# Per-chunk state product of an mLSTM in (128,32) column tiles, run together with the gather

## The chip, the cores and the metric

The kernel runs on one core of a Trainium2 chip. The metric is device time in microseconds (us) for one execution, taken as the median of three runs. TensorE is called PE, VectorE DVE, ScalarE ACT, GpSimd POOL; SP is SyncE, whose queue issues nearly all DMAs. "L902" is line 902 of the kernel before.

## The reference

An mLSTM layer (4 batches, 8 heads, 768 steps, head size 40) feeds a gated feed-forward network over 3072 tokens (320 to 1536 to 320):

```
for t in range(S):
    m_new = maximum(f[t] + m, i[t])
    C = exp(f[t] + m - m_new) * C + exp(i[t] - m_new) * outer(v[t], k[t])     # 40 x 40 per head
    n = exp(f[t] + m - m_new) * n + exp(i[t] - m_new) * k[t]
    y[t] = sigmoid(o[t]) * (C @ q[t]) / maximum(abs(n . q[t]), 1)
x = y laid out as (batch * step, head * 40)
out = (sigmoid(x @ w_gate) * (x @ w_val)) @ w_out
```

## The kernel before

The 768 steps are taken in 6 chunks of 128 tokens. A chunk c of a batch b is a unit, number 4c + b, 24 in all. Within a unit the recurrence is three matrix products. The *scores* (`b` in the order, L771/L776) are k·q per head, 128x128, which DVE multiplies with a decay matrix (`bm`, L782). The *gather* (`c`, L754) is scores times v: 8 heads, each cut by `by_columns` into four matmuls whose 32 columns of weights lie in one of the four column tiles of the array, 32 matmuls in all, with 41 columns of v each (40 and a column of ones for the normaliser n). *Into* (`ci`, L797) is q times the state that the chunks before left; it is faded (`cf`, L801) and added to the gather (`cs`, L810), and normalisation and the output gate follow (`cg` to `cx`).

The state of a batch is `cst[:, b]`, three groups of three, three and two heads. In each group the state stands as a block-diagonal matrix of 120x123 (the last 80x82), so that one *into* matmul serves a whole group. At the end of a unit of chunks 0 to 4 (20 units) it is brought up to date, in `st_e`:

- `z` (L902): three matmuls, v against the weighted k, give 120x123, 120x123 and 80x82 into a PSUM bank of their own, "cs". The products of different heads lie beside the diagonal blocks.
- `zm` (L913 on ACT, one piece per head column, or L917 on DVE): copies them out and multiplies with a mask `rmask` that keeps the blocks on the diagonal.
- `zd` (L896, POOL or DVE): the old state times the chunk's decay `cdec`; `za` (L922): the masked product is added. Both come in two parts (two groups, and the last).

The weighted k is `kt` times the last column of the decay matrix (`bk`, L757). From unit 8 on q and k go another way to PE: DVE flips them (`a`), splits them into a high part (`ah`, L697/L699) and a low part (`al`, L702), SP writes those to DRAM scratch (`as`, L706), reads q back as the weights of *into* (`aq`, L713, three transfers `qk`) and both back as stacked operands of the scores (`s`, L741). The decay matrices come from DRAM too (`ld`, L482).

The feed-forward takes 128 tokens at a time. All operands are split in a high and a low part in fp32r. Its up matmuls (`t`, `pg`, L951: 256 or 512 columns) fill PSUM, ACT and DVE make tanh and product (`ta` L964, `tg` L967), these are split again (`th` L972/L974, `tl` L978), and the down matmuls (`p`, `po`, L989, 320 columns) follow.

Nothing is scheduled while the kernel runs: all steps are put under keys, and a string ORDER lists the keys. Steps are issued in that order, each on its engine, and an engine runs its steps in that order alone. PSUM banks of the attention steps alternate between two; each is free again when its reader is done.

Of the kernel before, what the change touches and what calls it, by code (L numbers as in the profile page):

```python
# [9 lines left out]
F32 = mybir.dt.float32  # L10
F32R = mybir.dt.float32r
# [112 lines left out]
d1 w3b gc dy0 iq w3d wrf g dx1 lv2 a2.0 w3e w5a dy1 w7a g t0 w5b ah2.0 t0 lq4 t0 w5b t0 e2a w5b z0 t0 w7b t0*2 w7b
w5d a3.0 g e2m t0 zm0.0 t0 ah3.0 t0*5 zm0.1 w6a t0 w7b / a3.1 g ta0 w5e t0 w4f a2.2 ah3.1 gcs bk2 t1 tg0 t1*3 w6b
lo2 t1 th0 t1 v3 h0 t1 g t1 e3 t1*2 w6b t1*3 h0c t1 tl0 lo3 p0 t1 w6b t1 w4a / b2.0 ah2.2 w4b p0 ta1 p0 w4b b2.2
w7d g w4b p0 w7e t2 bm2.0 w6d t2 w7f t2*3 tg1 lv3 t2 e3a p0 bm2.2 b2.1 w5f w6e ld4 a3.2 w8a bm2.1 t2 e3m t2*2 ct2
t2 ah3.2 c2 th1 w8b w4d v6 bk3 b3.1 cg2 cv2 tl1 t2 cv2 t2 bm3.1 t2 w9a t2 p1 t2 w4e cv2 ct3 t2 / b3.0 cr2 ta2 w8b
cx2 p0 w9b b3.2 bm3.0 p1*2 bm3.2 t3*2 w8b z2 w9b w8d w8f p1 zm2.0 d2 zm2.1 w9b t3 w8e t3 dx2 tg2 c3 w9f w9d dy2 lk4
t3 w9e cg3 p1 gs t3*2 th2 cv3 z3 cv3 wvf gc w11a cv3 tl2 t3*2 w6f cr3 t3 zm3.1 t3*2 w11b lq5 t3 zm3.0 t3 cx3 t3 g  # L130
d3 lk5 t3 ta3 p2*2 dx3 p1 tg3 p2*2 w12a g p2 dy3 p2 k0 th3 t4 w12b t4*2 w11b k0c t4 ie w13a tl3 t4*2 w11b t4*2 e4
t4*5 p3 t4 w13b t4 w12b t4 a4.2 w13b ta4 p3 w12b p3 ah4.2 a4.1 w13b t5 w12d w14f t5 aq4.2 t5 tg4 t5 w12f t5 a4.0
ah4.1 w11d t5 lv4 w12e v5 t5*2 th4 t5 ld5 t5 w11e t5 ah4.0 t5*2 w10a lo4 t5*2 tl4 p4*2 w10f ci4 w10b ta5 aq4.0 e4a
p4 t5 p4 w10b p4 t6 tg5 t6 p4 w10b t6 w13d t6 e4m lo5 t6*3 cf4 t6 w10d t6*2 b4.2 th5 t6*2 w15a t6 bk4 lq6 tl5 t6*3
p5 bm4.2 p3*2 w10e p3 v4 p5 ta6 k0 b4.0 tg6 k0d t7 th6 t7 k0d t7 w13e w14a t7*2 tl6 t7 bm4.0 t7 w18a t7 p5 t7 w14b
t7*2 aq4.1 t7 p5 t7*2 k0d t7 w18b t7 p5 w14b ta7 p5 / a5.0 w18b z4 w14b ah5.0 w18b t8 w13f b4.1 g w18d w14d w15b t8
w18e lk6 e5a t8 tg7 t8 w18f t8 th7 t8 w14e zm4.0 p6*2 bm4.1 zm4.1 t8 w15f p6 w16a w15b t8 lq8 p6 t8 w15b e5 t8 gs
t8 w16b t8*2 tl7 t8*2 / h1 ta8 c4 h1c w16b*2 p6 v7 t8 p7*2 cs4 e5m a5.2 t9 tg8 ah5.2 t9 w17a p6 p7 t9 th8 w17b t9
w17b t9 w15d aq5.0 t9*2 w17b t9*2 tl8 w17d w17f t9*2 w11f w15e / a5.1 t9 gs ah5.1 t9 cv4 bk5 ct4 t9 w16f aq5.1 p7
cv4 w16d p7 cg4 p7 gs t9 cv4 p8 t9 cr4 ta9 w17e p8*3 w22a / a6.0 tg9 t10 ah6.0 p8 b5.0 w22b w19a w16e t10*2 th9 t10  # L140
w22b t10 w22b p8 t10 w19b k1 w22f tl9 p8 ld7 k1c t10 w22d bm5.0 p8 ld6 t10*2 w19b w21a t10*3 w21b t10*2 w22e t10 p9
w19b p9 w20a t10 w21b / k1 w19f ta10 p9 w20b p9 lq10 p9*2 zd4.0 w19d p8 lv5 p8 w20b p9 w19e p9 tg10 lo7 p8 p9 p8 p9
w20b t11 th10 t11*2 a8.0 w20d b5.1 tl10 w24a t11 bm5.1 t11*2 w20e t11*3 ah8.0 p10 w21b t11 p10*3 w21d w20f p10 t11
w24b p10 lk7 p10 w21e k1d p10 t11 k1d t11 k1d cx4 t11*3 al8.0 ta11 p9*2 / ci5 w23a zd4.1 aq5.2 t12 w25a cf5 a6.2
t12 tg11 zd5.1 t12*3 w23b th11 t12 w25b t12 ah6.2 ct5 t12 w23b t12 e6 w24b t12 w23b d4 w24b b5.2 w27f tl11 t12 w24d
w23f t12 w23d t12 w25b t12 bm5.2 t12 w23e lq7 p11 dx4 t12 ta12 p11 p10 dy4 w24e p11 ct7 p11*2 tg12 w26a p11*2 p10
zd5.0 p10 p11 w26b p11 th12 aq6.0 / c5 t13 cs5 ld8 a6.1 za4.1 p10 as8.0 ah6.1 p11 cv5 w25b t13 w27a t13*2 za4.0
w25d t13 tl12 t13 / z5 w25e w27b p12 t13 zm5.1 lk9 t13 p12 as8.3 t13 w29a t13 w27b t13 cg5 t13 cv5 t13 cv5 t13 cr5
p12*3 w27b p12 cx5 p11 w26b p11 w27d w24f t13 zm5.0 p12 as8.2 w26b ci6 w27e ta13 as8.1 aq6.2 p12 w26d lo6 t13 t14*2
tg13 t14 d5 w26e t14 dx5 t14 lq11 t14 za5.0 th13 t14 za5.1 t14 lo8 w29b w28a t14 cf6 t14*2 tl13 t14*2 aq6.1 t14 aq8  # L150
t14 lq9 w28b t14 w29b ta14 p12 aq8 p13 zd6.0 a7.2 w28b p13 lv6 ah7.2 p13 tg14 e6a p12 t15 lv9 t15 dy5 p12 p13*2
a9.1 p13 e7a lq12 / b6.0 e6m w28b p12 b6.1 ah9.1 bk6 e8 th14 p13*2 t15*2 al9.1 t15 bm6.1 t15 e7 t15 w29b t15 tl14
# [24 lines left out]
p30 aq11 e12a p30 tg32 p30 lo11 t33*2 th32 t33*2 s11 zm10.1 t33 a12.1 p31 tl32 p31 s11 p31 p32 s11 p32 ci10 as12.1
# [1030 lines left out]
```

## Time and profile before

| what | value |
|---|---|
| median of three runs | 515.25 us (515.25 to 515.4) |
| span of the profiled execution | 511.8 us |
| own time of that execution (taken as the median) | 515.25 us, 3.45 us of it outside the span |
| PE busy | 503.7 us, 4671 matmul records |
| DVE, ACT, POOL busy | 318.6, 200.8, 164.3 us |
| mean DMA rate | 148 GB/s |

The span is what the profiler's rows cover; an execution's time contains some us before and behind it. An fp32 matmul stands in the trace as two records, so the gather's 32 matmuls are 64 records. Matmuls are pipelined: a record's duration runs from its start to its result, and the next starts before that. What a matmul costs PE is therefore the distance from its start to the next one's start. The chain of waits follows the execution back from its last instruction, at each step to what released it.

### The profile page before, as it was taken

The page shows a single profiled execution, that of the slowest core. Times are in us where ns is not written, and L with a number is a line of the kernel's source. Part 1 is how long each engine was busy: PE and PEld are TensorE (multiplying, and loading weights), DVE is VectorE, ACT ScalarE, POOL GpSimd, SP SyncE. Part 2 cuts the span into 40 slices and gives each one's busy share as a digit, 9 for nine tenths or more (in the row PEclk, how much of TensorE's full clock was granted, in tenths as well). Part 3 has the DMA queues.
Part 4 walks back from the last instruction along what each step waited for, and adds up shares of the span by engine and source line. Part 5 has one row for each costly group of instructions (what it writes and reads, how often), then busy time and mean ns, then how long its engine had stood idle before and what let it go on. Part 6 is the DMA issues. An engine that isn't in the chain of part 4 may idle for free.

```text
span 511.8 us, 12224 instructions
## 1 busy us (share of the span) xinstructions
PE 503.7 (98%) x4671; PEld 458.4 (90%) x4671; DVE 318.6 (62%) x767; ACT 200.8 (39%) x530; POOL 164.3 (32%) x226
## 2 busy tenths in 40 slices
PE   7899999999999999999999999999999999999997
PEld 6788988889999999988888888888888888999997
DVE  8899998997647667565867366676444434442222
ACT  5987765674423332353332322213432411222321
POOL 3563334557730231342225322432241311101111
PEclk9999999999999999999999999999999999999999
DMA  9997768789889695977887788769759730000000
GB/s 196 240 274 192 200 192 221 168 141 189 191 179 172 136 216 119 199 150 156 186 161 180 146 189 195 160 127 190 165 118 198 155 87 5 27 28 1 28 0 27
DMA packets 227578, 75.55 MB, mean 148 GB/s; under 512 B 207040, under 2 KB 215424, under 8 KB 227520
## 3 DMA queue, kind: packets, MB, share of 16 engines
q1 hardware_dynamic: 226432, 74.51, 66.4%
q8 instruction: 37, 0.61, 0.5%
q10 hardware_dynamic: 1088, 0.26, 0.3%
q14 instruction: 21, 0.17, 0.1%
HBM read 57.61 MB, written 17.14 MB: 146 GB/s over the span
## 4 chain that ended last, share of the span: by engine, by line
PE 94%; DVE 3%; DMA 1%; issue 0%; ACT 0%; SPq 0%; DVEq 0%; ACTq 0%
PE pg L951 53%; PE po L989 25%; PE av L754 3%; PE in L797 3%; PE s L776 2%; PE s L771 2%; PE cs L902 2%; PE xt L867 1%; DVE gin L1178 1%; DMA gin<-in_f_gate_dram 1%; DMA st<-in_moe_w_val_dram 1%; PE s L1105 0%; PE pt L639 0%; DVE dc L548 0%; DVE x L842 0%
## 5 line engine op out<-in xcount | busy, mean ns | idle before, releaser
L964 ACT ACTIVATE sg<-pg 128x256 f32<-128x256 f32 (+1 forms) x103 | 48.3, 469 | 221.5 <-PE pg L951 214.8
L967 DVE SCALAR_TENSOR_TENSOR sg<-sg,pg 128x256 f32<-128x256 f32 (+1 forms) x103 | 53.7, 522 | 106.1 <-ACT sg L964 62.7
L951 PE MATMUL pg<-xh,wh 128*128 128x256 f32 (+1 forms) x412 | 112.2, 336 | 0.0
L951 PE MATMUL pg<-xl,wh 128*128 128x256 f32 (+1 forms) x412 | 109.6, 332 | 0.1
L951 PE MATMUL pg<-xh,wl 128*128 128x256 f32 (+1 forms) x412 | 106.2, 329 | 0.0
L978 POOL TENSOR_TENSOR gl<-sg,gh 128x256 fp32r<-128x256 f32 (+1 forms) x51 | 48.9, 958 | 178.2 <-ACT gh L972 61.3
L989 PE MATMUL po<-ol,gh 128*128 128x320 f32 x288 | 87.6, 316 | 0.0
L989 PE MATMUL po<-oh,gh 128*128 128x320 f32 x288 | 87.6, 315 | 0.0
L989 PE MATMUL po<-oh,gl 128*128 128x320 f32 x288 | 86.9, 318 | 0.0
L951 PEld LDWEIGHTS pg<-xl,wh 128*128 128x128 f32 x412 | 70.5, 188 | 6.7 <-DVE xl L880 0.3
L951 PEld LDWEIGHTS pg<-xh,wl 128*128 128x128 f32 x412 | 69.2, 188 | 5.4
L951 PEld LDWEIGHTS pg<-xh,wh 128*128 128x128 f32 x412 | 70.0, 188 | 4.3 <-ACT sg L964 0.5
L951 PE MATMUL pg<-xl,w 128*128 128x256 f32 (+1 forms) x206 | 60.7, 331 | 0.0
L989 PEld LDWEIGHTS po<-oh,gl 128*128 128x128 f32 x288 | 53.2, 188 | 3.2
L989 PEld LDWEIGHTS po<-oh,gh 128*128 128x128 f32 x288 | 53.3, 188 | 3.0
L989 PEld LDWEIGHTS po<-ol,gh 128*128 128x128 f32 x288 | 53.3, 188 | 2.8
L951 PE MATMUL pg<-xh,w 128*128 128x256 f32 (+1 forms) x206 | 54.4, 329 | 0.0
L782 DVE TENSOR_TENSOR d<-s,d 128x384 f32<-128x384 f32 (+1 forms) x66 | 33.1, 506 | 23.1 <-PE s L776 20.3
L972 ACT ACTIVATE gh<-sg 128x256 fp32r<-128x256 f32 (+1 forms) x58 | 28.8, 497 | 42.5 <-DVE sg L967 33.4
L490 ACT ACTIVATE d<-d,at 128x128 f32<-128x128 f32 x136 | 42.8, 390 | 0.0
L951 PEld LDWEIGHTS pg<-xl,w 128*128 128x128 f32 x206 | 36.7, 188 | 2.2
L951 PEld LDWEIGHTS pg<-xh,w 128*128 128x128 f32 x206 | 35.1, 188 | 2.8
(153 smaller groups left out, 712.9 us busy)
## 6 DMA issues: line engine op xcount, KB each, us to landing
d<-mscr SPq DMA_DIRECT2D x22, 512.0 KB
k<-in_k_dram SPq DMA_DIRECT2D x24, 160.0 KB
v<-in_v_dram SPq DMA_DIRECT2D x24, 160.0 KB
o<-in_o_gate_dram SPq DMA_DIRECT2D x24, 160.0 KB
st_o<-in_moe_w_out_dram SPq DMA_DIRECT2D x12, 320.0 KB
scr0q<-qt SPq DMA_DIRECT2D x32, 120.0 KB
scr1q<-qt SPq DMA_DIRECT2D x32, 120.0 KB
out_dram<-ob SPq DMA_DIRECT2D x24, 160.0 KB
```

What stands on the lines that cost most here:

```text
L490: nc.scalar.activation(d[:, h, :], d[:, h, :], AF.Exp, bias=at[:, c, b * H + h : b * H + h + 1], scale=-1.0)
L754: nc.tensor.matmul(dst[xs], lhs[:, xs], rhs, start=True, stop=True)
L771: nc.tensor.matmul(ps[g][:, :nh, :], sop[u][:r, g, 0, :], sop[u][:r, g, 1 : 1 + nh, :], start=True, stop=True)
L776: nc.tensor.matmul(ps[g][:, m, :], ks[: 3 * D, h0 + m, :], qs[: 3 * D, h0 + m, :], start=True, stop=True)
L782: nc.vector.tensor_tensor(x, ps[g][:, :nh, :], x, ALU.mult)
L797: nc.tensor.matmul(pi[:, h0 : h0 + nh, :], qk[u][:r, g, :], cst[:r, b, g, : nh * DA], start=True, stop=True)
L951: nc.tensor.matmul(pg[x], w[:, a, fs] if a < 2 else w[:, fs], y[c][:, a, n0:n1], start=first, stop=a == 2 and y is xl)
L964: nc.scalar.activation(sg[0], pg[0], AF.Tanh, scale=0.5)
L967: nc.vector.scalar_tensor_tensor(sg[0], sg[0], 1.0, pg[1], ALU.add, ALU.mult)
L972: nc.scalar.activation(gh[u][:, :nt], sg[0], AF.Copy)
L978: E('gl0' if c == 0 else 'gl', f'tl{n}').tensor_tensor(gl[u][:, :nt], sg[0], gh[u][:, :nt].bitcast(F32), ALU.subtract)
L989: nc.tensor.matmul(po[t], g[c, j, t0][:, (t - t0) * P : (t - t0 + 1) * P], o[:, j, :], start=j == 0 and first, stop=j == NF - 1 and last)
```

## The change

The state is kept differently. `pair_state(b)` is 128 x 4 x 41: heads (0,3,6,2) stand in the upper 64 rows, heads (1,4,7,5) in the lower 64, four side by side; 24 of every 64 rows hold leftovers of neighbouring heads that nothing reads. The product becomes `outer`: 16 matmuls, each with 32 columns of the weighted k as weights and 41 columns of v, which write 32 rows of one head into one column tile. There are no products of different heads that must be masked.

For chunks 1 to 4 (16 units) `outer` follows in the same step as the gather's 32 matmuls and writes behind them in the same PSUM bank. For chunk 0 (4 units) it stays a step of its own, and a copy (`zm`) takes it out. `zd` is one operation of 128x164 on POOL, `za` one on DVE which reads PSUM directly; masks and their temporaries are gone.

*Into* still reads a block-diagonal matrix, now `cb`, which `zi` fills with zeros once (a POOL memset of 128x1476). `moved` copies the diagonal blocks there from the pair state: four transfers on SP per unit, 80 in all, `zs` in the order (two of 40x3x41, two of 40x41). `cdec` is made by copies, without the mask. In ORDER the first 113 words stand as before and the others are laid anew.

```diff
+PAIRS = ((0, 3, 6, 2), (1, 4, 7, 5))
+MOVES = ((0, 0, 0, 0, 3), (1, 1, 0, 0, 3), (2, 0, 3, 0, 1), (2, 1, 3, 1, 2))
...
-    cst = const.tile([P, B, 3, 3 * DA], F32, name="cst")
+    cb = const.tile([P, B, 3, 3 * DA], F32, name="cb")
...
+    def outer(u, dst):
+        for p in range(4):
+            for w in range(2):
+                for e in range(2):
+                    h = PAIRS[e][p]
+                    x0 = h * D - e * (64 - D) + 32 * w
+                    r0 = 64 * e + 32 * w
+                    nc.tensor.matmul(dst[r0 : r0 + 32, p, :], kt[u].rearrange("p h d -> p (h d)")[:, x0 : x0 + 32],
+                                     vt[u][:, h, :], start=True, stop=True)
...
-                nc.tensor.matmul(pi[:, h0 : h0 + nh, :], qk[u][:r, g, :], cst[:r, b, g, : nh * DA], start=True, stop=True)
+                nc.tensor.matmul(pi[:, h0 : h0 + nh, :], qk[u][:r, g, :], cb[:r, b, g, : nh * DA], start=True, stop=True)
...
         def gather():
-            t["pv"] = pv = bank(c, b, [P, H, DA], "av")
+            x = bank(c, b, [P, 12, DA], "av")
+            t["pv"], t["po"] = pv, po = x[:, :H, :], x[:, H:, :]
             for h in range(H):
                 by_columns(pv[:, h, :], dm[u][:, h, :], vt[u][:, h, :], PARAM['AV'])
+            if 0 < c < NCH - 1:
+                outer(u, po)
+
+        def fade():
+            x = pair_state(b)
+            E('cd', f'zd{n}').tensor_tensor(x, x, cdec[:, c - 1, b].unsqueeze(2).broadcast_to([P, 4, DA]), ALU.mult)
+
+        def added():
+            x = pair_state(b)
+            nc.vector.tensor_tensor(x, x, t["po"], ALU.add)
...
+        def moved(j, e, p0, g0, g1):
+            nc.sync.dma_start(cb[j * D : (j + 1) * D, b, g0:g1, j * DA : (j + 1) * DA],
+                              pair_state(b)[88 * e : 88 * e + D, p0 : p0 + g1 - g0, :])
```

In the rows of the order below, numbers behind a name are chunk, batch and a buffer's number; `x2` means twice in a row.

**Unit 4 and its state product.** PE in the kernel before; `cs_1_0` is the product's bank, `av_1_0` the gather's, `pt` the transposes of the next unit's q and k:

```order
L989 MATMUL po3_0_987<-oh_109,gl_0_1_2_1024 128x320
L639 MATMUL pt0_1_1_1085<-ident_94,k_1_1_845 120x128
L644 MATMUL pt0_1_1_1085<-ident_94,qpad0_89 120x128
L902 MATMUL cs_1_0_1089<-v_1_0_939,k_1_0_793 120x123 x2
L902 MATMUL cs_1_0_1089<-v_1_0_939,k_1_0_793 80x82
L951 MATMUL pg0_0_4_0_1099<-xh_0_435,wh0_103 128x512
L771 MATMUL s1_1_0_1104<-kq_1_0_910 128x384
L951 MATMUL pg0_0_4_0_1099<-xh_0_435,wh0_103 128x512
```

PE in the changed kernel:

```order
L951 MATMUL pg0_0_4_0_1147<-xl_0_467,w20_103 128x512
L646 MATMUL pt2_1_1_1195<-ident_93,k_1_1_971 80x128
L651 MATMUL pt2_1_1_1195<-ident_93,qpad0_89 80x128
L761 MATMUL av_1_0_1198<-v_1_0_1064,d_1_0_837 32x41 x32
L629 MATMUL av_1_0_1198<-v_1_0_1064,k_1_0_856 32x41 x16
L951 MATMUL pg1_0_4_0_1171<-xl_0_467,w21_106 128x512
L989 MATMUL po3_0_1010<-ol_108,gh_0_2_2_1101 128x320
```

The three wide matmuls stood between transposes and the next tile's `pg`, in a bank of their own; now 16 narrow ones follow the gather's 32 with nothing between them.

**Unit 2, the gather behind the scores.** PE in the kernel before; `s0`, `s1` and `s2` are the scores of heads 0 to 2, 3 to 5, and 6 and 7:

```order
L771 MATMUL s1_0_2_631<-kq_0_2_431 128x384
L639 MATMUL pt2_0_3_638<-ident_94,k_0_3_364 80x128
L642 MATMUL pt2_0_3_638<-ident_94,qpad1_90 80x128 x2
L951 MATMUL pg1_0_2_0_645<-xh_0_435,wh1_106 128x256 x2
L951 MATMUL pg1_0_2_0_645<-xh_0_435,wl1_107 128x256 x2
L754 MATMUL av_0_2_653<-v_0_2_418,d_0_2_301 32x41 x32
```

PE in the changed kernel:

```order
L951 MATMUL pg0_0_2_0_630<-xl_0_467,wh0_101 128x256
L778 MATMUL s1_0_2_643<-kq_0_2_439 128x384
L951 MATMUL pg0_0_2_0_630<-xl_0_467,wh0_101 128x256
L778 MATMUL s2_0_2_653<-kq_0_2_439 128x256
L951 MATMUL pg1_0_2_0_661<-xh_0_443,wh1_104 128x256
L761 MATMUL av_0_2_665<-v_0_2_426,d_0_2_299 32x41 x32
L951 MATMUL pg1_0_2_0_661<-xh_0_443,wh1_104 128x256
```

The last scores ahead of the gather were `s1`, with three transposes and four `pg` matmuls behind them; now they are `s2`, with one `pg` matmul behind them.

**Unit 9, the weights of its *into*.** SP in the kernel before; `qk_2_1` are the three transfers of q, `scr0q` and `scr0k` writes to scratch for unit 10:

```order
L1009 DMA out_0_dram<-ob_0_1_2076 128x320
L706 DMA scr0q_85<-qt_2_2_2088 32x30x32 x2
L713 DMA qk_2_1_2202<-scr1q_87 40x3x128 x2
L706 DMA scr0q_85<-qt_2_2_2088 32x30x32
L713 DMA qk_2_1_2202<-scr1q_87 40x2x128
L706 DMA scr0q_85<-qt_2_2_2088 32x30x32
L1009 DMA out_0_dram<-ob_0_2_2250 128x320
```

SP in the changed kernel:

```order
L720 DMA qk_2_1_2462<-scr1q_87 40x3x128 x2
L713 DMA scr0k_86<-kt_2_2_2345 32x20x32
L923 DMA cb_109<-cst_412 40x41
L713 DMA scr0k_86<-kt_2_2_2345 32x20x32
L923 DMA cb_109<-cst_412 40x3x41
L923 DMA cb_109<-cst_412 40x41
L720 DMA qk_2_1_2462<-scr1q_87 40x2x128
L748 DMA qs_2_1_2524<-scr1q_87 80x1024
L748 DMA qs_2_1_2524<-scr1q_87 40x1024
```

The third transfer of `qk_2_1` now stands behind two writes of unit 10's k and three moves of state; before it stood behind a write of unit 10's q.

## Rows read from the trace of the kernel before

**Rows 1.** The page: span, busy time by engine, chain by engine.
```profile
span 511.8 us, 12224 instructions
...
PE 503.7 (98%) x4671; PEld 458.4 (90%) x4671; DVE 318.6 (62%) x767; ACT 200.8 (39%) x530; POOL 164.3 (32%) x226
...
PE 94%; DVE 3%; DMA 1%; issue 0%; ACT 0%; SPq 0%; DVEq 0%; ACTq 0%
```

**Rows 2.** Windows view: length, busy by engine (instructions), clock, DMA share, GB/s.
```profile
30.00:130.00 100.00, 99.43 (x962) 86.90 (x962) 90.39 (x222) 65.32 (x181) 47.13 (x60) 1.00 0.81 195
```

**Rows 3.** Waits view of PE: us in total, times, longest us.
```profile
PE pwarm0x L1052 <- DVE warm L1178: 1.3, 1, 1.3
```

**Rows 4.** PE timeline, state product of unit 5: start us, us, instructions.
```profile
132.28 0.73 PE L902 MATMUL cs<-v,k 128*120 128x123 f32 x6
132.81 0.37 PE L951 MATMUL pg<-xh,wh 128*128 128x256 f32 x1
133.01 0.32 PE L989 MATMUL po<-oh,gl 128*128 128x320 f32 x1
133.16 0.28 PE L951 MATMUL pg<-xh,wh 128*128 128x256 f32 x1
133.28 0.40 PE L951 MATMUL pg<-xh,wl 128*128 128x256 f32 x2
```

**Rows 5.** PE timeline, a gather; below it the gather's line: busy us, mean ns.
```profile
144.94 0.28 PE L951 MATMUL pg<-xl,w 128*128 128x256 f32 x1
145.15 0.82 PE L754 MATMUL av<-v,d 128*32 128x41 f32 x64
145.90 0.51 PE L951 MATMUL pg<-xh,wh 128*128 128x256 f32 x2
146.24 0.31 PE L989 MATMUL po<-oh,gl 128*128 128x320 f32 x1
...
L754 PE MATMUL av<-v,d 128*32 128x41 f32 x1536 | 19.9, 202 | 0.4 <-DVE d L1110 0.3
```

**Rows 6.** Tile views of state and product: count, ns min/median/max, starts, forms.
```profile
L896 POOL TENSOR_TENSOR cst<-cst,cdec x21: 315/592/794, 87.2 to 356.5; 80x82 f32<-80x82 f32 x11, 120x246 f32<-120x246 f32 x10
L922 DVE TENSOR_TENSOR cst<-cst,ct x17: 191/406/780, 95.6 to 405.0; 80x82 f32<-80x82 f32 x9, 120x246 f32<-120x246 f32 x8
...
L913 ACT ACTIVATE ct<-cs,rmask x38: 280/298/333, 62.9 to 370.0; 80x41 f32<-80x41 f32 x20, 120x82 f32<-120x82 f32 x18
```

**Rows 7.** PE timeline, a group of two heads' scores and its neighbours.
```profile
54.00 0.60 PE L771 MATMUL s<-kq 80*128 80x256 f32 x2
...
54.67 0.40 PE L951 MATMUL pg<-xh,w 128*128 128x256 f32 x2
```

**Rows 8.** PE timeline, three transposes and the product behind them.
```profile
142.77 0.52 PE L867 MATMUL xt<-ident,x 128*128 128x128 f32 x3
143.04 0.36 PE L951 MATMUL pg<-xh,wh 128*128 128x256 f32 x1
```

**Rows 9.** Lines by form: busy us, mean ns, idle before them and releasers.
```profile
L964 ACT ACTIVATE sg<-pg 128x256 f32<-128x256 f32 x62 | 23.8, 385 | 103.0 <-PE pg L951 96.8 <-PE s L776 2.7 <-DVE gl L978 1.8
L967 DVE SCALAR_TENSOR_TENSOR sg<-sg,pg 128x256 f32<-128x256 f32 x62 | 25.8, 416 | 64.6 <-ACT sg L964 40.5 <-PE pg L951 24.1
L699 DVE CAST kt<-kr 128x320 fp32r<-128x320 f32 x9 | 3.4, 380 | 0.1
L702 POOL TENSOR_TENSOR kt<-kr,kt 128x320 fp32r<-128x320 f32 x9 | 7.9, 881 | 5.6 <-ACT kt L697 4.9 <-DVE kt L699 0.4 <-DMA qs<-scr0q 0.3
```

**Rows 10.** SP's timeline of DMA issues: start us, us in the queue's issue.
```profile
137.60 0.34 SPq L706 DMA_DIRECT2D scr0q<-qt  x1
138.00 0.47 SPq L713 DMA_DIRECT2D qk<-scr1q  x1
...
146.02 3.36 SPq L482 DMA_DIRECT2D d<-mscr  x1
```

**Rows 11.** Chain of waits, opening: start us, us from issue to landing.
```profile
0.81 2.96 DMA gin<-in_f_gate_dram
```

More of the change, by code (lines that the diff above doesn't have):

```diff
@@ L124 @@
[L124 to L128, printed above, removed]
@@ L272 @@
+p99 p98 ta100 p98*2 p99 t101*6 tg100 t101*3 th100 t101*7 tl100 p99*4 ta101 t102 tg101 th101 t102*5 oh20 t102*6 tl101
+t102*4 p100*6 p101*2 o20 p101 ta102 tg102 th102 p101*2 p102*2 tl102 p102 oh22 o22 p101 p102*3 oh23 o23
 """
 GROUPS = ((0, 3), (3, 3), (6, 2))
+PAIRS = ((0, 3, 6, 2), (1, 4, 7, 5))
+MOVES = ((0, 0, 0, 0, 3), (1, 1, 0, 0, 3), (2, 0, 3, 0, 1), (2, 1, 3, 1, 2))
 @with_exitstack
@@ L385, in mlstm_then_gated_ffn_kernel @@
     mend = const.tile([BH, NCH + 1], F32, name="mend")
-    ones = const.tile([BH, L], F32, name="ones")
     rmask = const.tile([P, 3], F32, name="rmask")
@@ L402, in mlstm_then_gated_ffn_kernel @@
     m0 = t1_tile([P, L], "m0")
-    mm = const.tile([P, L], F32R, name="mm")
-    pick2 = const.tile([P, BH], F32R, name="pick2")
+    first = two.tile([P, B * 4 * DA], F32, tag="cst", name="first", bufs=1)
+    mm = first[:, :L].bitcast(F32R)
+    pick2 = first[:, L : L + BH].bitcast(F32R)
+    ones = first[:BH, 2 * L : 3 * L]
     def gate_max(key, c):
@@ L456, in mlstm_then_gated_ffn_kernel @@
     sel = t1_tile([P, P], "sel")
-    cdec = const.tile([P, NCH, B, 3], F32, name="cdec")
+    cdec = const.tile([P, NCH - 2, B, 4], F32, name="cdec")
     def gates_turn(key, c0, c1):
@@ L620, in w_more, with pair_state @@
             w_dma(*q[m])
-    cst = const.tile([P, B, 3, 3 * DA], F32, name="cst")
+    cb = const.tile([P, B, 3, 3 * DA], F32, name="cb")
+    cst = {}
+    def pair_state(b):
+        if 0 not in cst:
+            cst[0] = two.tile([P, B, 4, DA], F32, tag="cst", name="cst", bufs=1)
+        return cst[0][:, b]
+    def outer(u, dst):
[7 more added lines that the diff above has]
+                                     vt[u][:, h, :], start=True, stop=True)
     def bank(c, b, shape, name):
@@ L817, in st_c @@
         put(f"c{n}", gather)
+        if 0 < c < NCH - 1:
+            put(f"zd{n}", fade)
+            put(f"za{n}", added)
         norm(n, u, lambda: t["pv"])
@@ L889, in st_e @@
         ps = {}
-        def cv(g0, ng, r, w):
-            return cst[:r, b, g0 : g0 + ng, :w]
-        def fade(g0, ng, r, w):
-            x = cv(g0, ng, r, w)
-            E('cd', f'zd{n}.{g0 // 2}').tensor_tensor(x, x, cdec[:r, c, b, g0 : g0 + ng].unsqueeze(2).broadcast_to([r, ng, w]), ALU.mult)
-        def outer():
-            ps[0] = bank(c, b, [P, 3, 3 * DA], "cs")
-            for g, (h0, nh) in enumerate(GROUPS):
-                r = nh * D
-                nc.tensor.matmul(ps[0][:r, g, : nh * DA], kt[u][:, h0 : h0 + nh, :].rearrange("p h d -> p (h d)"),
-                                 vt[u][:, h0 : h0 + nh, :], start=True, stop=True)
@@ L920, in added, with alone @@
-        def added(g0, ng, r, w):
-            x = cv(g0, ng, r, w)
-            E('ca', f'za{n}.{g0 // 2}').tensor_tensor(x, x, ps[1, g0], ALU.add)
-        put(f"z{n}", outer)
-        for part in ((0, 2, 3 * D, 3 * DA), (2, 1, 2 * D, 2 * DA)):
-            x = f"{n}.{part[0] // 2}"
-            put(f"zm{x}", own, *part)
-            if c > 0:
-                put(f"zd{x}", fade, *part)
-                put(f"za{x}", added, *part)
+        def alone():
+            ps[0] = bank(c, b, [P, 4, DA], "cs")
+            outer(u, ps[0])
@@ L932, in mlstm_then_gated_ffn_kernel @@
+        for x in MOVES:
+            put(f"zs{n}", moved, *x)
     gh, gl, po = {}, {}, {}
@@ L1134, in opening @@
         gates_of("gc", 1, 2)
+    put("zi", nc.gpsimd.memset, cb, 0.0)
     tiles = []
```

325 lines of the change are left out of this document (155 added, 170 removed).

## The prediction

> **What bounds the kernel now.** I read the page first. PE is busy for 503.7 of 511.8 us, every other engine for less than two thirds of that, and 94% of the chain that ended last lies on PE [rows 1]. So a microsecond counts only if it is PE's own, or if PE waits for it. Next I read the windows view for the stretch in which the most attention work lies: from 30 to 130 us PE is busy for 99.43 of 100 us, at a granted clock of 1.00 (the upper level, 2.4 GHz), while DVE is busy for 90.39 and the DMA engines for 0.81 of the time [rows 2]. The waits view then shows what is left to win by better order: PE's longest own wait is 1.3 us, behind the first warm-up [rows 3], and the seven rows of that view sum to 4.6 us. The clock is full and the waits are small, so the time follows PE's instructions, measured from one start to the next in PE's timeline.
>
> **What the old product costs.** In the timeline around unit 5 the product starts at 132.28 and the next up matmul at 132.81, so it holds PE for 0.53 us. That up matmul then takes until 133.01, 0.20 us, where one of the same shape a little later takes from 133.16 to 133.28, 0.12 us [rows 4]. The cost is 0.53 + 0.08 = 0.61 us, and it goes in all 20 units.
>
> **What the new product costs.** The gather is the nearest thing in the trace: the same kind of matmul, 32 of them, 64 records. From its first start to its last result it takes 0.82 us, and one record lasts 0.202 us, so the 64 starts are spread over 0.62 us, 9.8 ns apart. The next up matmul starts 0.75 us after the first record. The entry shows in the matmul ahead (144.94 to 145.15, 0.21 in place of 0.12), the exit in the two behind (145.90 to 146.24, 0.34 in place of 0.24) [rows 5]. The whole gather thus costs 0.75 + 0.09 + 0.10 = 0.94 us. In chunks 1 to 4 the 16 new matmuls stand right behind it, so entry and exit are paid already and 32 more records come in: at 9.8 ns 0.31 us, at 0.75/64 = 11.7 ns 0.375 us. I take 0.33, near the lower end, as records in the middle of a run are what is added. 16 units x (0.61 - 0.33) = **4.5 us saved**, between 3.8 and 4.8.
>
> In chunk 0 the 16 matmuls stand alone and pay both ends: 0.94 - 32 x 0.0098 = 0.63 us against 0.61. I take nothing for these 4 units; if the shorter run drained faster they could give 0.1 us each.
>
> **The other engines.** Masks, two-part fades and two-part adds go: 70 instructions of 0.23 to 0.42 us for the masks, and 64 for fades and adds of which the rows show 0.315 to 0.794 us on POOL and 0.191 to 0.780 on DVE [rows 6]. In their place come 16 fades of 164 elements on POOL (between the 82- and the 246-element forms, so some 0.4 to 0.6 us), 16 adds on DVE in the same way (0.3 to 0.5), and 4 copies on ACT of about 0.3. I cost all of it at nothing: it lies beside PE, which has work in hand. The cover is the distance of four units between one chunk's `za` and the next chunk's *into* of the same batch; without it an add and the moves behind it would end late at one *into*. A lighter DVE gains nothing either, since PE hardly waits for it.
>
> **The moves.** 80 issues are added to SP's queue. The nearest rows are a scratch write, 0.34 us, and a read of q, 0.47 us [rows 10]; 80 of them are 27 to 38 us of a queue that also has to place decay matrices and scores' operands in time. Where data arrive well ahead this costs nothing. I looked through the new order for inputs that come close, and found two.
>
> First, **unit 9's *into***. On DVE the product of tile (1,6) stands ahead of the high part of unit 10's k; SP holds the third transfer of unit 9's q behind two writes of that k and three moves. From the last up matmul of tile (1,6) the chain is 0.28 us for that matmul, 0.385 for tanh, 0.416 for the product, 0.380 for the high part, 0.881 for the low part [rows 4, 9], 2.4 us with handoffs rounded up. Five issues ahead at 0.47 give 2.35, and the transfer itself lands at the earliest some 2.96 us after its issue if it is as slow as the gates' load in the opening [rows 11]. That is 7.7 us. PE meanwhile has that matmul (0.12), three transposes (0.27, from 142.77 to 143.04 [rows 8]), gather and product (0.94 + 0.33), 31 up matmuls at 0.12 (3.72) and 13 down matmuls at 0.147 (1.91; the row is 133.01 to 133.16): 7.3 us. So PE would wait **0.4 us**. With issues of 0.34 it is nothing; if one issue is held as the decay matrix at 146.02 was, for 3.36 us [rows 10], it is about 3.3.
>
> The Trainium skill, page "DMA: Bandwidth & Descriptors", section "Anatomy of one DMA — SWDGE (gpsimd) path", puts the fixed part of a DMA at about 2.0 us. By that figure, an estimate here since it was fitted on another path, the chain would be 6.7 us, the wait would vanish, and the sum would be 0.4 better.
>
> Second, **unit 2's gather**, now one up matmul behind the last scores. Those take 0.60 us from start to result, the DVE product behind them 0.42 (the row of a product of the same shape [rows 9]), 1.02 together. In PE's timeline such scores and two up matmuls fill 54.00 to 54.67 [rows 7]; less one of the two, 0.55 us is what PE has to do. It waits **0.5 us**, between nothing and 1.0 (if DVE comes a whole operation late).
>
> **The sum.** -4.5 + 0.4 + 0.5 = -3.6. The profiled execution is taken at 515.25, the median of the runs: its span of 511.8 and 3.45 around it, which the change leaves alone. 515.25 - 3.6 = **511.7 us**. With the bounds above this case runs from 510.5 to 513.9.
>
> **Rivals.**
>
> *All of the gain arrives.* Unit 9's data are in time, DVE is ahead at unit 2 because 70 mask operations are gone, and no new wait arises: 515.25 - 4.5 to 4.8 = 510.4 to 510.8, or 509.4 if the new order also takes about 1 us out of PE's 4.6 us of waits. For it: DVE loses work in its fullest stretch. Against it: the two short distances stand in the order.
>
> *The queue eats it.* Three *into* or score inputs come late by the four moves ahead of them: 3 x 4 x 0.34 to 0.47 = 4.1 to 5.6 us, which gives 514.8 to 516.4, about 515.5. For it: the queue gets longer by a fifth (424 issues before). Against it: the seven rows of PE's waits name DVE and ACT, never a DMA.
>
> *Slower, by SP.* Each move waits for `za`, which waits for PE, and every load behind it waits too. The price is four issues, 1.4 to 1.9 us, wherever a load has no slack. The point from which it decides is 0.3 us of lateness per unit of chunks 1 to 4 (4.5/16), or three units at the full price. With half of the 16 units late it is 8 x 1.9 - 4.5 = +10.7, 526 us. Against it: SP already had an issue held for 3.36 us [rows 10], and PE did not feel it.
>
> *The tiles run one after another*, so that the change doesn't do what it says. The old product passes 2 x 328 columns in 0.53 us, 0.81 ns each; 32 records of 41 columns at that rate are 1.06 us, 0.45 more than the 0.61 that goes, and 20 units make +9.0, 524 us. Against it: the gather's 64 records would then take 2.1 us, and they take 0.75. What is left for it: the gather's four tiles share their 41 columns of v, while `outer` gives two different heads to its two halves. The Trainium skill, page "TensorEngine Tiling (Array Packing)", section "Performance Considerations", says that each matmul has an overhead of some 60 cycles, so that narrow ones don't pay. By that figure, estimated one after another at 25 ns, 32 records are 0.8 us and the change would lose 0.2 us per unit, about 519 us. The trace disagrees with this reading: 9.8 ns from start to start.
>
> **How the numbers follow.** About 0.2%, 1.0 us, can be told from no change, so faster is below 514.2 and slower above 516.3. My forecast has 0.50, the whole gain 0.17, the queue 0.18, SP 0.09, tiles in sequence 0.06. Faster: 0.50 + 0.17 + two late units in place of three 0.03 = 0.70; same: 0.14 of the queue case; slower: 0.09 + 0.06 + the queue's last 0.01 = 0.16. The range goes from 509.4, the whole gain with its waits, to 516.4, the end of the queue case, and leaves out 0.15.
>
> **What would show it.** Right: PE has 520 records more (20 x 32 in, 20 x 6 out) and yet less busy time; the run of 96 records takes about 1.15 us; the waits view has small rows at the *into* and gather of two units, under 1 us together; no `cs` bank in chunks 1 to 4. The queue case would show *into* lines with releaser DMA on `qk` or `cb`; SP's case the same in most units, with moves held in SP's timeline behind DVE; the sequence case a run of 1.7 us or more. I am wrong if PE's waits grow by over 2 us, or if the up matmuls show another interval than 0.12.

## The result, and the profile after

The changed kernel takes 519.62 us (median of six, 519.17 to 522.89), the kernel before 515.24 (514.27 to 515.4) beside it: 4.4 us less. The ratio, which is taken over all runs and not from the two medians, is 1.0108, 95% interval 1.0084 to 1.0131. It is slower, where 511.7 us was forecast; the range ended at 516.4. In the runs below, too, a time is a median, and the ratio behind it, with its interval, is to runs of the kernel before taken beside it.

The page of the changed kernel, the lines that answer to [rows 1]:

```profile
span 517.6 us, 13246 instructions
...
PE 501.0 (97%) x5191; PEld 453.0 (88%) x5191; DVE 311.6 (60%) x738; ACT 190.5 (37%) x483; POOL 154.5 (30%) x207
...
PE 71%; DMA 9%; DVE 7%; SPq 6%; ACT 3%; issue 3%; POOL 1%; ACTq 0%; DVEq 0%
```

The span grew by 5.8 us. PE's busy time fell by 2.7 us (503.7 to 501.0), and its idle time grew by 8.5 (8.1 to 16.6). PE carries 71% of the chain where it carried 94. In every run since, a profiled execution's time stands 1.7 to 1.9 us above its span, so the profile of before, with its span of 511.8, probably belongs to an execution of some 513.6 and not to the median, and the 3.45 us outside the span that the text above took are too many. The forecast is not moved by this, as it adds a difference to the median; but where two profiles are compared, that of before lies some 1.7 us below its median. So the spans differ by 5.8 us and the medians by 4.4.

The windows view shows where the idle time lies (length; PE, PEld, DVE, ACT and POOL busy, with instructions; clock; DMA share; GB/s). Two rows of the kernel before, beside [rows 2]:

```profile
0.00:30.00 30.00, 25.79 (x283) 21.67 (x284) 25.82 (x73) 22.64 (x63) 14.53 (x32) 1.00 1.01 229
...
130.00:230.00 100.00, 100.00 (x1067) 97.55 (x1066) 62.37 (x162) 35.51 (x99) 32.79 (x47) 1.00 0.81 168
```

and the changed kernel:

```profile
0.00:30.00 30.00, 23.90 (x324) 19.82 (x324) 25.39 (x67) 20.11 (x52) 14.67 (x33) 1.00 0.92 220
30.00:130.00 100.00, 97.42 (x1102) 82.89 (x1101) 87.87 (x212) 61.03 (x165) 45.30 (x55) 1.00 0.78 185
130.00:230.00 100.00, 96.82 (x1197) 95.07 (x1198) 59.86 (x152) 32.53 (x85) 32.44 (x45) 1.00 0.86 178
230.00:330.00 100.00, 98.56 (x919) 85.40 (x922) 56.82 (x120) 30.18 (x74) 27.45 (x33) 1.00 0.78 155
```

Outside PE's busy time lie 6.1, 2.6, 3.2 and 1.4 us. Before it was 4.2 in the first 30 us, 0.6 between 30 and 130 us and nothing from 130 to 430. The clock is 1.00 in all of them: the upper level, as before. PE's waits in the changed kernel, the larger rows, against [rows 3]:

```profile
PE in L804 <- DMA qs<-scr1q: 1.6, 1, 1.6
PE s L783 <- DMA qs<-scr0q: 1.3, 1, 1.3
PE pwarm0x L1052 <- DVE warm L1179: 1.3, 1, 1.3
PE s L783 <- DMA qs<-scr1q: 1.2, 1, 1.2
...
PE pt L646 <- DMA k<-in_k_dram: 0.9, 1, 0.9
...
PE av L761 <- DVE qc L666: 0.6, 1, 0.6
PE pt_cdec L455 <- DVE d L789: 0.6, 1, 0.6
...
PE s L778 <- DVE kq L666: 0.5, 1, 0.5
```

Two kinds of waits are new: for DMAs (the *into* of unit 9, the scores of units 8 and 15, a load of k in the opening), and for DVE, 0.3 to 0.6 us each, between 30 and 100 us. No row names the add, which now has to read the gather's bank before the bank is free again, so a wait of that kind is not seen.

What the change does on PE came out nearly as worked out. A gather with its product, the line that answers to [rows 5]:

```profile
148.26 0.82 PE L761 MATMUL av<-v,d 128*32 128x41 f32 x64
148.89 0.49 PE L629 MATMUL av<-v,k 128*32 128x41 f32 x32
149.31 0.50 PE L951 MATMUL pg<-xh,wh 128*128 128x256 f32 x2
```

From the first gather record to the next up matmul it is 1.05 us, where the gather alone took 0.75: 0.30 for the 16 matmuls (0.33 forecast). Of the 16 such runs in PE's timeline 13 take 1.04 to 1.05 us and three 1.12 to 1.23, so the mean is 0.32. The tile views of state and moves, against [rows 6]:

```profile
L923 SPq DMA_DIRECT2D cb<-cst x80: 724/798/3012, 32.6 to 422.0; - x80
```

```profile
L821 POOL TENSOR_TENSOR cst<-cst,cdec x16: 455/465/909, 61.7 to 353.0; 128x164 f32<-128x164 f32 x16
L825 DVE TENSOR_TENSOR cst<-cst,av x16: 285/317/326, 71.0 to 364.2; 128x164 f32<-128x164 f32 x16
```

Fade and add cost what was taken (0.47 and 0.32 us). A move holds SP's queue for **0.80 us** in the median and for 0.72 at the least, not 0.34 to 0.47: 80 of them are 64 us.

### The profile page after: what moved, and what is told of

The parts are those of the page before. It is cut to its first block, busy times and chain, and to the rows that moved or that the text cites. A ratio compares the mean times of both kernels' runs of the same rounds, so it can differ in the third digit from the quotient of the medians.

```text
span 517.6 us, 13246 instructions
## 1 busy us (share of the span) xinstructions
PE 501.0 (97%) x5191; PEld 453.0 (88%) x5191; DVE 311.6 (60%) x738; ACT 190.5 (37%) x483; POOL 154.5 (30%) x207
## 4 chain that ended last, share of the span: by engine, by line
PE 71%; DMA 9%; DVE 7%; SPq 6%; ACT 3%; issue 3%; POOL 1%; ACTq 0%; DVEq 0%
PE pg L951 42%; PE po L989 20%; PE av L761 2%; SPq L923 2%; PE s L783 2%; DMA st<-in_moe_w_val_dram 2%; PE in L804 2%; DMA qs<-scr1q 2%; DMA st<-in_moe_w_gate_dram 1%; DMA qs<-scr0q 1%; SPq L713 1%; DMA out_dram<-ob 1%; PE xt L888 1%; SPq L748 1%; DVE dc L535 1%
## 5 line engine op out<-in xcount | busy, mean ns | idle before, releaser
L978 POOL TENSOR_TENSOR gl<-sg,gh 128x256 fp32r<-128x256 f32 (+1 forms) x51 | 50.1, 982 | 233.6 <-ACT gh L972 82.9
L951 PE MATMUL pg<-xh,wh 128*128 128x256 f32 (+1 forms) x412 | 110.1, 338 | 0.6 <-ACT sg L964 0.5
L951 PE MATMUL pg<-xh,wl 128*128 128x256 f32 (+1 forms) x412 | 107.7, 331 | 0.0
L989 PE MATMUL po<-oh,gl 128*128 128x320 f32 x288 | 85.7, 312 | 0.0
L951 PE MATMUL pg<-xl,w 128*128 128x256 f32 (+1 forms) x206 | 61.9, 334 | 0.0
```

The costliest lines, as they stand in the source:

```text
L951: nc.tensor.matmul(pg[x], w[:, a, fs] if a < 2 else w[:, fs], y[c][:, a, n0:n1], start=first, stop=a == 2 and y is xl)
L978: E('gl0' if c == 0 else 'gl', f'tl{n}').tensor_tensor(gl[u][:, :nt], sg[0], gh[u][:, :nt].bitcast(F32), ALU.subtract)
L989: nc.tensor.matmul(po[t], g[c, j, t0][:, (t - t0) * P : (t - t0 + 1) * P], o[:, j, :], start=j == 0 and first, stop=j == NF - 1 and last)
```

## The experiments

Three theories were tried. *Queue*: the moves make loads late. *Order*: the new order stands too close to its producers, with or without moves. And, from the results on, *DVE*: PE waits where DVE is full.

**1. No moves.** The 80 `zs` words are taken out; *into* reads zeros.

```diff
-zs0
...
-zs19
```

> Leaves out the 80 moves of state (the block-diagonal copy stays zero, so the part of the output that comes from earlier chunks is missing); all else is the changed kernel. Queue theory (the moves, 0.80 us each in SP's queue in place of the 0.34 to 0.47 that the sum used, make loads late): PE's waits for DMAs, 5.2 us in the changed kernel, go, and the time is 514 to 515.5. Order theory (the newly laid order puts producers too close ahead of PE, with or without moves): 518.5 to 520.

It took 514.78 us, 1.0011 of before (0.9989 to 1.0032): the moves cost the changed kernel 4.8 us by the medians (some 3.4 to 6.6 by the two intervals). The queue theory's number is met, but the kernel only comes back to the time before, not below it. Its windows, and the one larger wait for an attention operand that is left:

```profile
30.00:130.00 100.00, 97.21 (x1070) 81.94 (x1072) 88.46 (x212) 60.90 (x164) 46.30 (x53) 1.00 0.75 183
130.00:230.00 100.00, 98.60 (x1255) 96.81 (x1242) 60.31 (x153) 33.88 (x89) 32.88 (x48) 1.00 0.84 179
230.00:330.00 100.00, 99.96 (x992) 87.23 (x991) 57.37 (x122) 28.73 (x69) 28.25 (x35) 1.00 0.76 155
```

```profile
PE s L780 <- DMA qs<-scr0q: 1.0, 1, 1.0
```

From 130 to 330 us PE's idle time falls from 4.6 to 1.4 us. From 30 to 130 us it stays (2.8 here, 2.6 with moves): that loss is not the moves'. The late inputs of units 9 and 15 are gone; unit 8's scores still wait 1.0 of their 1.3 us, so that input is late for the most part without any move.

**2. Moves on ACT's queue.**

```diff
-            nc.sync.dma_start(cb[j * D : (j + 1) * D, b, g0:g1, j * DA : (j + 1) * DA],
+            nc.scalar.dma_start(cb[j * D : (j + 1) * D, b, g0:g1, j * DA : (j + 1) * DA],
```

> The 80 moves are issued from ACT's queue in place of SP's, at the same places of the order. Queue theory: SP's queue is as short as before and the DMA waits go, 514 to 516, if 80 issues on ACT (37% busy) don't hold up tanh; if they hold it up by 0.8 us each wherever PE is close behind, 520 and more. Order theory: 519 to 520.

538.63 us, 1.0433 (1.0382 to 1.0483). A move holds ACT for 0.80 us too, and PE waits longer for operands of which ACT makes a part:

```profile
L923 ACTq DMA_DIRECT2D cb<-cst x80: 727/798/1452, 31.1 to 445.7; - x80
```

```profile
PE s L783 <- DMA qs<-scr0q: 6.5, 2, 3.3
```

This tells nothing for or against SP's queue, as the price of the other queue covers it.

**3. The change in the order of the kernel before.** Words of the product become a change of bank, `zd` and `za` stand by the gather, the moves are spread.

```diff
-z5 zm5.1 zm5.0 za5.0 za5.1
+/
...
+zd5
...
 cs5
+za5
...
+zs5
...
+zs5
```

> The whole change, but with the order of the kernel before: the product's words are taken out, fade and add stand next to the unit's gather, and the four moves of a unit are spread evenly between its add and the next chunk's use. Order theory: the saving of 4.7 us arrives, 510.5 to 512. Queue theory: the moves make loads late here too, 515 to 517.

518.93 us, 1.0095 (1.0064 to 1.0127): worse than either theory had it. PE waits for DMAs (first two rows) and for ACT's tanh:

```profile
PE in L811 <- DMA qk<-scr0q: 1.4, 1, 1.4
...
PE s L790 <- DMA qs<-scr1q: 1.3, 1, 1.3
...
PE pg L958 <- ACT sg L971: 1.3, 5, 0.5
```

In its timeline the product of chunk 0 can be read by itself:

```profile
39.76 0.50 PE L636 MATMUL cs<-v,k 128*32 128x41 f32 x32
40.20 0.42 PE L996 MATMUL po<-oh,gh 128*128 128x320 f32 x1
```

0.44 us to the next start; with the entry and exit of [rows 5], 0.09 and 0.10, it is 0.63, as forecast, against 0.61 for the old product.

**4. Moves alone, in the kernel before.** 80 transfers of the same sizes to a spare tile (which takes in a constant's tile as well), spread as in run 3.

```diff
-    ones = const.tile([BH, L], F32, name="ones")
+    spare = const.tile([P, L], F32, name="spare")
+    ones = spare[:BH, :]
...
+            nc.sync.dma_start(spare[j * D : (j + 1) * D, g0 * DA : g1 * DA].rearrange("p (g e) -> p g e", e=DA),
+                              cst[j * D : (j + 1) * D, b, g0:g1, j * DA : (j + 1) * DA])
```

> The kernel before, with 80 transfers of the same sizes from the state to a spare tile, placed as in the run before this one; nothing reads them. Queue theory: about 4 to 5 us of new waits for DMAs, 519 to 521. Order theory: 515 to 516.

514.57 us, 0.9996 (0.9979 to 1.0013): nothing. Each takes SP just as long, and no wait of PE names a DMA; the longest but the warm-up's is for DVE:

```profile
L925 SPq DMA_DIRECT2D spare<-cst x80: 721/813/3471, 32.2 to 414.4; - x80
```

```profile
PE pt L639 <- DVE kq L659: 1.1, 1, 1.1
```

So 65 us more in SP's queue are free here, with PE's work as before and the moves in places with room. The queue theory in its plain form falls: their number alone costs nothing.

**5. Moves spread in the new order.** Only the `zs` words stand elsewhere.

```diff
-zs4*2
...
+zs4
...
+zs4
```

> The changed kernel with its 80 moves at other places of the order: a unit's four stand evenly between its add and the next chunk's use, as in the run where they cost nothing. If their places decide: about 515 (the run without them took 514.8). If their number does, whatever the place: 519 to 520.

517.90 us, 1.0063 (1.0043 to 1.0083): between the two. From 230 us on PE waits no more, and one wait for a DMA is left, larger than before:

```profile
PE s L783 <- DMA qs<-scr0q: 2.9, 1, 2.9
```

That is unit 8's first scores again; even spreading had put moves ahead of their operands (run 12 takes three of them away).

**6. Unit 9's q first.**

```diff
+zs5 aq9
...
 as10.5
...
 zs6
...
 as10.6
...
 zs7
-zs5
...
-aq9
 ci9
```

> Two words of the changed kernel's order are moved: the last transfer of unit 9's q and the last move of unit 5's state stand ahead of the writes of unit 10's k, with which they shared the queue. If the chain of the prediction (tile (1,6), unit 10's k, issues of 0.8 us) is the cause of the 1.6 us wait at unit 9's into: that wait goes, 518 to 518.4. If something else holds that input, the wait stays and the time is 519.5.

517.83 us, 1.0061 (1.0037 to 1.0086), 1.8 us less than the changed kernel by the medians (0.7 to 4.2 by the intervals). The row of *into* is gone from PE's waits, the other two remain:

```profile
PE s L783 <- DMA qs<-scr0q: 1.1, 1, 1.1
PE s L783 <- DMA qs<-scr1q: 1.1, 1, 1.1
```

The row named `qs<-scr1q`, transfers that *into* doesn't read and that are issued right behind its own; their place is the same here, so it was `qk`. That this transfer stood behind five issues is thereby shown as the cause of the wait. What stands ahead of these issues, from tile (1,6) to unit 10's low part, is read from the timelines (below) and was not changed in a run.

**7. Moves on POOL's queue.**

```diff
-            nc.sync.dma_start(cb[j * D : (j + 1) * D, b, g0:g1, j * DA : (j + 1) * DA],
+            nc.gpsimd.dma_start(cb[j * D : (j + 1) * D, b, g0:g1, j * DA : (j + 1) * DA],
```

> The 80 moves are issued from POOL's queue (30% busy), at the same places of the order. If SP's queue is what they cost: DMA waits of PE go, 514.5 to 516. If an issue holds POOL for a microsecond or more and its low parts come late: 517 to 525.

523.22 us, 1.016 (1.0144 to 1.0176). A move takes POOL 0.65 us, and one arrives 2.4 us too late at an *into*:

```profile
L923 POOL DMA_DIRECT2D cb<-cst x80: 512/649/897, 26.9 to 429.5; - x80
```

```profile
PE in L804 <- DMA cb<-cst: 2.4, 1, 2.4
```

**8. Run 3 without moves.**

```diff
-zs0
...
-zs19
```

> The change with the order of the kernel before, but without the moves (the part of the output from earlier chunks is missing). If the queue ate the gain there too: 510.5 to 512, the full saving. If the rest of the change (fade, add, the gather's bank held until the add) makes waits of its own in that order: 514 to 516.

517.22 us, 1.004 (1.0025 to 1.0055), above both forecasts. In that order the moves cost 1.7 us by the medians (1 to 4.6 by the intervals), and some 7 us are lost without them (517.2 against 514.8, the kernel before beside it, less 4.9):

```profile
PE s L786 <- DMA qs<-scr1q: 1.6, 1, 1.6
PE pg L954 <- ACT sg L967: 1.3, 5, 0.4
...
PE in L807 <- DMA qk<-scr0q: 0.9, 1, 0.9
```

So transfers come too late though no move stands ahead of them. How much of this is due to the places that I gave fade and add isn't told apart. From 30 to 130 us PE is idle for 1.4 us in this order, with moves or without, where the new order has 2.6 to 2.8; from 130 to 330 us it is 3.3 us without moves, where the new order has 1.4. Neither order is free of waits, and they have them at different places.

**9 and 10. PE's order changed by hand.** Run 6, and matmuls of the network pulled ahead of the late steps (one place of each is shown in run 9's edit).

```diff
+t20*8
 / b8.2
...
-t20*8
```

> On top of the two moved words at unit 9, PE's order is mended at three other late waits of the changed kernel: 8 up matmuls are pulled ahead of the first scores of unit 8, 10 up and down matmuls ahead of those of unit 15, one down matmul ahead of unit 9's gather. If distance in the order is what was missing, their 1.5, 1.4 and part of 0.4 us go too: 514.5 to 515.5. If the data are late because the DMA engines are full, the waits come back behind the pulled work or at other units: 517 to 518.

```diff
+t6 t7*2 p5 t7
 / b4.0
...
+p8*4
 / k1
...
+t13 p11*5
 c5
```

> As the run before, and the same at three waits for DVE in the first 130 us: 5 matmuls ahead of unit 4's first scores (0.56 us), 4 ahead of the decay's transposes at 85 us (0.84), 6 ahead of unit 5's gather (0.78). If those waits are of the order's making: 512.5 to 513.5, faster than the kernel before. If DVE is the bound there, PE waits for it at the next place: 514.5 to 515.5.

Run 9 took 516.61 us, 1.0032 (1.002 to 1.0044): 1.2 less than run 6, of the 3 that were named: between the two forecasts. In its profile the waits at units 8 and 15 are down to 0.4 and 0.5 us, and a new one of 1.5 us for tanh stands behind unit 9's gather (that execution took 520.2, well above the median). Run 10 took 519.29, 1.0085 (1.007 to 1.01), 2.7 more than run 9, which neither of its forecasts had. Matmuls pulled ahead made PE wait for the tanh of its own tiles instead, here in run 10:

```profile
PE pg L951 <- ACT sg L964: 2.2, 4, 1.1
```

In these two runs the work pulled into one wait was missing at the place that it came from.

**11. The old kernel with less work.** `z`, `zm` and `za` of chunks 1 to 4 are taken out of the kernel before.

```diff
-z5 zm5.1 zm5.0 za5.0 za5.1
+/
```

> The kernel before without the state product, its masks and its adds in chunks 1 to 4 (16 units; the state only fades, so the output from chunk 2 on is not the reference's). It takes 16 x 0.61 = 9.8 us from PE and adds nothing. If a microsecond of PE is a microsecond of time, as the prediction had it: 505 to 505.5. If the order leaves little distance, so that saved work turns into waits: 507.5 to 511.

508.46 us, 0.9873 (0.9858 to 0.9888): 6.6 us of the 9.8 arrive. From its page:

```profile
span 506.0 us, 11911 instructions
...
PE 496.2 (98%) x4575; PEld 448.7 (89%) x4575; DVE 311.5 (62%) x734; ACT 192.0 (38%) x492; POOL 155.8 (31%) x211
```

PE is idle for 506.0 - 496.2 = 9.8 us, where it was 8.1, and busy for 7.5 us less, where the product had cost it 9.8. That it did cost 9.8 shows in the timeline of before: in 13 of the 16 units the product takes 0.52 to 0.53 us to the next start, and the matmul behind it 0.08 to 0.09 more than usual. The missing 2.3 us of busy time belong to waits too. In run 11's timeline 16 matmuls of attention and network stand ahead of an idle gap, where 8 did, and such a matmul holds PE for some 0.18 us more than its usual interval, as nothing overlaps its end; that is 1.4 us. The other 0.9 us are in intervals between up and down matmuls that grew without a gap. So with nothing added anywhere, a third of what PE saves (9.8 less 6.6) comes back as waits and what they cost around them. This is the plainest measurement of the premise of the prediction.

**12. Moves spread, and unit 8's operands freed.** Run 5, with three moves taken from ahead of unit 8's operands, and 8 up matmuls ahead of its scores.

```diff
-zs5
...
-zs6
...
-zs5
...
 ci8
...
+zs5
...
+zs6 t20*8
 / b8.2
...
+zs5
```

> The changed kernel with its moves spread evenly, three of them taken from the queue ahead of unit 8's operands to behind its into, and 8 up matmuls pulled ahead of unit 8's first scores. The even spread left one late wait for a DMA, 2.9 us at those scores. If the moves can be hidden wholly by their places: that wait goes and the time is 514.5 to 515.5, as without any move (514.8). If there is always an input that they make late: 517 to 518. Faster than the kernel before, below 514, neither theory expects, since the waits for DVE in the first 130 us stay.

514.91 us, 0.9991 (0.9981 to 1.0001): what the kernel without moves takes. Places, with those 8 matmuls, are worth 4.7 us; the two are not told apart. At unit 8's scores no DMA is named any more, but PE is still idle there for 0.8 us (first row; `issue` means that the profile shows nothing it waited for). The waits for DVE between 30 and 130 us are those of the changed kernel, row for row:

```profile
PE s L783 <- issue: 0.8, 1, 0.8
...
PE av L761 <- DVE qc L666: 0.6, 1, 0.6
...
PE pt_cdec L455 <- DVE d L789: 0.5, 1, 0.5
...
PE s L778 <- DVE kq L666: 0.5, 1, 0.5
```

**13 and 14. Work taken off DVE.** Run 12 with copies out of PSUM given to ACT (`ah3.2`, `ah4.1`, `ah6.2`), then also two low parts to POOL (`tl4`, `tl11`).

```diff
-'ah3.2': 'v', 'ah4.1': 'v', 'ah6.2': 'v'
+'ah3.2': 'a', 'ah4.1': 'a', 'ah6.2': 'a'
```

> The kernel of the run before this one (moves hidden, 514.9), with five copies out of PSUM given from DVE to ACT: those of unit 3's third, unit 4's second and unit 6's third transposes. The first and the last were the ones that PE waited for, at unit 2's scores (0.5 us) and unit 5's gather (0.6). If DVE, 92% busy between 30 and 100 us, is what gives back the rest of the gain: these two waits go and the time falls by 1.0 to 1.5, to 513.5 to 514. If PE's waits there come from the order alone, whichever engine copies: 514.5 to 515.2.

```diff
-'tl4': 'v', 'tl11': 'v'
+'tl4': 'p', 'tl11': 'p'
```

> As the run before, and two low parts (of 256 and 512 columns, 0.43 and 0.69 us on DVE) are made on POOL in place of DVE, at 53 and 95 us. If DVE is the bound: another 0.3 to 0.8 us less, 513 to 513.7. If POOL's longer operation makes the down matmuls wait: 514.5 to 516.

516.26 us (1.0033, 1.0013 to 1.0053) and 519.17 us (1.0086, 1.0068 to 1.0103): both slower than run 12, and above every forecast. The 0.5 us at unit 2's scores went, but two others of 0.5 us came close by, and at unit 5's gather PE now waits longer, for ACT (run 13):

```profile
PE av L761 <- ACT qc L668: 2.0, 1, 2.0
```

In ACT's timeline the copy starts at 98.38 us, behind an operation that waited for DVE until 96.81, a tanh and two more; on DVE, in run 12, it started at 97.13. So the copy is late by what stands ahead of it, as these two timelines read; no run takes that away. That DVE's load gives back the rest of the gain is not shown, and these two runs speak against it. No run was faster than the kernel before with the whole computation in it.

## Why the prediction was wrong

**PE's own work: right.** 16 units save 0.61 - 0.30 us each and four lose 0.02, 4.9 in all (4.5 forecast, and 4.5 too with the three longer runs counted as they stand). There are 520 records more, and the tiles don't run in sequence. The overhead of some 60 cycles per matmul that the Trainium skill gives (page "TensorEngine Tiling (Array Packing)", section "Performance Considerations"), taken one after another, made an estimate of 0.8 us for the 32 records; the trace contradicts that estimate: they took 0.30.

**"A microsecond counts only if it is PE's own": right one way, wrong the other.** A microsecond of PE's is not a microsecond of time. Run 11 gave 0.67 for one, with nothing added. The small waits before (4.6 us) did not mean that producers had time in hand.

**The moves: the term that was mis-sized.** The price came from two single rows, 0.34 and 0.47 us [rows 10]; it is 0.80 (0.77 for 40x41, 0.83 for 40x3x41, medians of 40). The place was right. SP's timeline in the changed kernel, at unit 9:

```profile
150.03 0.31 SPq L713 DMA_DIRECT2D scr0k<-kt  x1
150.38 1.08 SPq L923 DMA_DIRECT2D cb<-cst  x1
151.51 1.37 SPq L713 DMA_DIRECT2D scr0k<-kt  x1
152.93 1.62 SPq L923 DMA_DIRECT2D cb<-cst  x2
154.59 0.51 SPq L720 DMA_DIRECT2D qk<-scr1q  x1
```

and, there, POOL's low part of unit 10's k and PE (in brackets, the idle time before and what released it):

```profile
149.13 0.87 POOL L709 TENSOR_TENSOR kt<-kr,kt 128x320 fp32r<-128x320 f32 x1 [1.22 <-DVE kt L706]
...
154.84 0.31 PE L989 MATMUL po<-ol,gh 128*128 128x320 f32 x1
156.71 0.87 PE L804 MATMUL in<-cb,qk 120*128 120x123 f32 x6 [1.56 <-DMA qs<-scr1q]
```

The chain ran as written: unit 10's low part is done at 150.0, five issues take from 150.03 to 154.59, 4.56 us in place of 2.35; *into* starts 2.12 us after the last issue began, where 2.96 was taken. The three moves are 2.70 us of the 4.56; one write of k was held for 1.37, by what the rows don't say. The wait was 1.6 us, not 0.4. The Trainium skill's 2.0 us for the fixed part of a DMA (page "DMA: Bandwidth & Descriptors", section "Anatomy of one DMA — SWDGE (gpsimd) path") lies near that 2.12, though it was fitted on another path.

**"I looked for inputs that come close, and found two": the step that failed most.** Unit 9 was one. At unit 2 the wait came one step earlier, 0.5 us for DVE ahead of the scores, and the gather itself lost another 0.24. But units 8 and 15 (1.3 and 1.2 us), a load of k (0.9), and the waits for DVE at four other places were not seen. The two distances that were worked out took an issue at half its price, and only the operations of the chain itself, not all that stands in a queue. The sign of being wrong that the prediction gave, waits of PE that grow by over 2 us, came: its idle time grew by 8.5. The upper bound of 513.9 for "this case" does not follow from the bounds stated: 3.8 saved, 3.3 at unit 9 and 1.0 at unit 2 give 515.8.

**"I cost all of it at nothing", for DVE:** between 30 and 130 us DVE is busy for 87.87 us in place of 90.39, and still PE is idle for 2.6 us there in place of 0.6. DVE's load as a whole fell, so it is not that; that DVE's steps stand closer ahead of PE in the new order is the likely reason, not a shown one. For it: the same work has 1.4 us there in the old order (runs 3 and 8). Runs 10 and 13 only exchanged some of these waits for others.

**The rivals.** The queue rival gave the mechanism (three late inputs of 1.2 to 1.6 us, forecast 1.4 to 1.9 each) and about its price: run 1 puts it at 4.8 us (4.1 to 5.6 forecast). In part that is luck: two of the three inputs are the moves' doing, while unit 8's is late by 1.0 us without them. The time went past that rival because of a further 4.5 us, which no rival had. So: 515.2 - 4.9 + 4.8 + 4.5 = 519.6. Against the forecast of 511.7 the moves are 4.4 us more than the 0.4 that was taken, the other waits 4.0 more than the 0.5, and PE's own work 0.4 less. The 4.5 is what is left over when the other three are taken from the time, not a measurement by itself. Where it lies shows in the profile of run 1, which has no moves: PE is idle for 0.9 us more than before in the opening, 2.2 from 30 to 130 us, 1.4 from 130 to 330 and 0.5 behind. (These rows don't add up to the 4.5, as that profile lies 1.6 us above its median and that of before below, and as waits cost more than their rows.) The opening is no matter of the order alone: the change in the old order has 5.3 and 5.5 us there (runs 3 and 8), where the kernel before has 4.2.

A wait also costs more than its row says. In the timeline above the matmul ahead of *into* starts at 154.84 and *into* at 156.71, 1.87 us, of which 0.15 is the matmul's own interval. 1.72 went for a wait of 1.56, since matmuls that would have overlapped didn't. In PE's timeline 20 matmuls of attention and network stand ahead of a gap, where 8 did; together they hold PE for 1.6 us more, and intervals that grew without a gap for another 0.6. That accounts for the 2.2 us by which PE's busy time fell less than the 4.9 (by 2.7).

**What stays open:** whether another order could avoid the waits of the first 130 us, and why unit 8's input is late without moves. Pulling PE's work (run 10), copies on ACT (13) and low parts on POOL (14) each made it slower.

## What to carry to other kernels

When one engine is busy for 98% and shows hardly a wait, don't expect all of what is saved on it: here, measured once, two thirds arrived. Small waits may mean that producers are just in time. Whether an order laid again with measured prices would give the rest was not shown. Price a new kind of DMA by the issue of that kind, in a run that adds it alone, and remember that the cost lies in what stands behind it: 80 transfers of the same sizes cost nothing in the old kernel (run 4) and in run 12, 1.7 us in run 3 and 4.8 us in the changed kernel. Before moving work to another engine's queue, look at what is ahead of it there: the copy that PE waited for came later on the less busy engine.

## What was not expected of the hardware

Issuing one of these transfers, from SBUF to SBUF with runs of 164 bytes, held SP's queue for 0.80 us in the median, nearly the same for 40x41 as for 40x3x41 elements (6.4 and 19.2 KB; 0.77 and 0.83), and ACT's for as long; on POOL it was 0.65 (0.55 and 0.70). The shortest was 0.72 us on SP, where the shortest writes of q and k to DRAM scratch took 0.30 to 0.31 in the kernel before (their medians, 0.49 to 0.58, hold time in which they were held). Whether the runs of 164 bytes or the two ends in SBUF make the difference was not tried. With 80 such transfers more in SP's queue, no DMA came late to PE in the old kernel.
